# Logits read as pairs of neighbouring columns, six units with the one-table gate, and new instruction lists

## The chip, the core and the metric

The kernel runs on one NeuronCore of one Trainium2 chip. The metric is the device time of one execution in microseconds. Five engines work side by side, each through its own instruction list: PE multiplies matrices (its weight loads, PEld, overlap with it), DVE (VectorE), ACT (ScalarE) and POOL (GpSimd) work on rows, and SP issues the DMAs.

## The reference

A gated linear recurrence over 4 sequences of 5056 tokens with 256 channels, followed by a mixture of experts in which each of 32 slots (8 experts, 4 slots each) takes a weighted sum of all 20224 tokens:

```
a_t = exp(c * sigmoid(r_gate) * log(a_base))            # c = 8, a_base = sigmoid(a_param)
u   = sqrt(max(1 - a_t*a_t, 1e-6)) * sigmoid(i_gate) * x
y_t = a_t * y_(t-1) + u_t                               # over each sequence
logits = y @ phi                                        # 20224 x 32
d = softmax of logits over all tokens;  slot_input = d.T @ y
slot_out = relu(slot_input[e] @ w1[e]) @ w2[e]          # 8 experts, 256 -> 1024 -> 256
out = (softmax of logits over the 32 slots) @ slot_out  # 20224 x 256
```

All inputs and the output are fp32 in HBM: about 62 MB of x and gates, 17 MB of weights, 20.7 MB of output.

## The kernel before

The 20224 tokens are cut into 40 quads of 512 tokens (the last has 256), and the quads into 21 units: unit 0 is quad 0, units 1 to 19 hold two quads each (1024 tokens), unit 20 is quad 39. Units go by chunks of two, and units 0 to 17 pair up into groups of four (or three) quads for the softmax; units 18, 19 and 20 are groups of their own.

The loads put a quad into an `st` tile (gates) or half a `b` tile (x), a number of consecutive tokens in each partition. The recurrence needs channels in partitions, so everything is transposed on PE. For quad q, unit p, channel half h, group g the steps are, with the names of the instruction lists:

- SP: `Drq`, `Diq`, `Dxq` load the three inputs, `w1e` and `w2e` the weights, `ODg.j` writes output.
- `TRq` (PE, L742) transposes r_gate, `SRq` (ACT, L753) takes its tanh, `EXp.h` (ACT, L821) the exponential: a_t. `SQp.h` (POOL or DVE, L808) squares it, `RTp` (ACT, L844) takes the root.
- `SIq` (ACT, L766 or L768) is the input gate, `Uq` (POOL or DVE, L791) multiplies it with x, `TUp.h` (PE, L863) transposes the product into a PSUM pair, `STp.h` (DVE, L881) multiplies it with the root, `SCp.h` (DVE, L898) is the scan. y then stands in the unit's `b` tile, channels in partitions, token 8m+n of a two-quad unit in column 8m+n.
- `TYq` (PE, L921) transposes y back, eight 128x128 blocks for a quad, `YCq` (DVE L937 or ACT L935) copies it out of PSUM into a `yn` tile.
- `LGg.k` (PE, L980): the logits of a unit and channel half, four matmuls with 32 columns of phi as weights and y as the moving operand, into four strips of 32 partitions. `LEg` (DVE, L996) takes them out of PSUM with a running maximum, `LDg` (L1012, L1016) subtracts it, `TEg` (PE, L1027) transposes, `ESg` (ACT, L1036) is exp, `ACg.k` (PE, L1054) adds up the slot inputs over the tokens with y from `yn` as the moving operand, `AEg` (DVE, L1069) accumulates them.
- `CTg` (PE, L1428), `CMg`, `CSg`, `CEg`, `RRg`, `CNg`, `CHg`, `CLg` are the softmax over slots.
- When all tokens are scanned: `MX`, `MR`, `WJ`, `WE`, `W`, `SP`, `SL` merge the partial sums, `L1.e` and `L2.e` (PE, L1308 and L1356) are the experts, `SO` to `BD` (DVE, ACT) prepare slot_out, and then `HP`, `HE`, `OT` (PE, L1531), `OE` (DVE L1547 or ACT L1545) and `OD` make the output.

The input gate has kinds, one letter for each unit in `IV`. Kind S is a sigmoid, which needs a function table of its own on ACT; `U` multiplies it into the x tile and `TU` transposes that one tile. Kind E is tanh(i/2), which is in the table that the exponentials use; `U` multiplies it with x in the gate's own tile, and `TU` transposes both that tile and x and adds them up in PSUM (x + x tanh(i/2) is twice x sigmoid(i); the half goes into the root). So for E `TU` has 32 transposes of a unit for each two channel halves where S has 16, and the `st` tile of the gate is free after `TU`, where with S it is free after `U`. Kind P is tanh with a correction on POOL. There are 7 `st` tiles, which r_gate and i_gate share.

Nothing is ordered by chance: `ORDER` holds one list of step names for each engine, and each engine issues its steps in that order. A planner only assigns tiles and checks that the lists can run; the costs in `add(...)` calls don't reorder anything while `ORDER` is given. [...] `UD` and `SQD` say for which steps DVE may take over from POOL.

Of the kernel before, what the change touches and what calls it, by code (L numbers as in the profile page):

```python
# [17 lines left out]
P = 128  # L18
J = 4
# [10 lines left out]
IV = 'EEEESSSSPPESPSSSSSSSP'  # L30
# [43 lines left out]
SQD = 4  # L74
UD = 6
# [28 lines left out]
    ),  # L104
    "ACT": (
# [12 lines left out]
    ),  # L118
# [20 lines left out]
    ),  # L139
# [344 lines left out]
def kernel(  # L484
# [37 lines left out]
    def plen(p):  # L522
        return sum(qlen(q) for q in quads(p))
# [72 lines left out]
    def per_part(p):  # L596
        return plen(p) // P

    def token(v, p):
        return v.rearrange("c (p n) -> c p n", n=per_part(p))  # L600
# [1008 lines left out]
```

## Time and profile before

| | us |
|---|---|
| median of 3 runs (lowest, highest) | 310.09 (309.19, 310.15) |
| the profiled execution's own time | 310.56 |
| its span, first to last instruction | 308.8 |
| PE, DVE, ACT, POOL busy | 276.9, 252.1, 248.3, 201.8 |
| all inputs but weights loaded and scanned, merge done (SL) | about 232 |
| first output DMA issued | 255.2 |

The profile divides into three stages: up to 232 us the tokens are loaded, scanned and summed up; from 232 to 255 us the experts run, almost only on PE, and hardly any data is moved; from 255 us to the end the output is made and written. The busy time of an engine says little over the whole span, since each stage has its own limit; a row of a stage has to be read by itself. Quoted lines from the profile give times from the span's start; a group's row reads: line, engine, operation, output tile <- input tiles, shapes, count, then busy time and mean ns of one, then idle time before it and what ended it.

### The profile page before, as it was taken

How to read it: one execution, taken by the hardware profiler on the slowest of the kernel's cores; microseconds unless marked ns; L12 is line 12 of the kernel's file. 1: busy time of each engine (PE TensorE's matmuls, PEld its weight loads, DVE VectorE, ACT ScalarE, POOL GpSimd, SP SyncE). 2: the span in 40 equal slices, each digit the busy share in tenths (PEclk: the TensorE clock that was granted, in tenths of full speed). 3: DMA queues.
4: the chain of work that ended last, by engine and by line, in shares of the span. 5: the costliest groups of instructions: out<-in, count | busy, mean ns of one | idle time of the engine just before them, and what ended most of it. 6: DMA issues, size and time to landing. Idle time of an engine off the chain costs nothing.

```text
span 308.8 us, 6015 instructions
## 1 busy us (share of the span) xinstructions
PE 276.9 (90%) x2353; PEld 201.4 (65%) x2353; DVE 252.1 (82%) x295; ACT 248.3 (80%) x264; POOL 201.8 (65%) x149
## 2 busy tenths in 40 slices
PE   7989888978889999989889999999999989999960
PEld 6988676555556776766574567567654568788740
DVE  0275989899799899988999899999976988898620
ACT  5999999999999999899999999999460027755660
POOL 1542989888999996989597989793124656113200
PEclk9999999979999999999999999999997999999996
DMA  7999998999997677896988696799996008999996
GB/s 217 418 407 368 406 409 304 329 408 402 409 390 245 206 238 254 286 409 237 355 331 293 229 330 246 267 382 416 422 373 284 2 2 340 407 419 412 420 423 267
DMA packets 23776, 100.04 MB, mean 324 GB/s; under 512 B 2882, under 2 KB 2884, under 8 KB 19780
## 3 DMA queue, kind: packets, MB, share of 16 engines
q1 hardware_dynamic: 23744, 99.66, 84.2%
q8 instruction: 18, 0.29, 0.4%
q14 instruction: 10, 0.08, 0.1%
q10 hardware_dynamic: 4, 0.00, 0.0%
HBM read 78.94 MB, written 20.71 MB: 323 GB/s over the span
## 4 chain that ended last, share of the span: by engine, by line
PE 48%; DVE 22%; ACT 11%; POOL 7%; issue 5%; DMA 4%; ACTq 0%; DVEq 0%; POOLq 0%
PE one L980 9%; DVE b L898 8%; PE bank L1531 8%; PE pair L863 6%; PE pair L921 6%; DVE pair L881 5%; PE pair L742 5%; PE one L1531 4%; ACT b L753 3%; PE one L1054 3%; POOL b L791 3%; PE bank L1308 2%; ACT st L768 2%; POOL b L808 2%; DMA st<-in_r_gate_dram 2%
## 5 line engine op out<-in xcount | busy, mean ns | idle before, releaser
L808 POOL TENSOR_TENSOR b<-b 128x1024 f32<-128x1024 f32 (+2 forms) x38 | 68.8, 1833 | 20.5 <-ACT b L821 20.4
L791 POOL TENSOR_TENSOR b<-st,b 128x1024 f32<-128x1024 f32 (+1 forms) x29 | 67.7, 2347 | 12.3 <-DMA b<-in_x_dram 11.1
L881 DVE SCALAR_TENSOR_TENSOR pair<-b,pair 128x1024 f32<-128x1024 f32 (+2 forms) x42 | 48.3, 1156 | 7.5 <-PE pair L863 6.2
L742 PE MATMUL pair<-ident,st 128*128 128x128 f32 x316 | 44.0, 284 | 7.9 <-DMA st<-in_r_gate_dram 4.6
L742 PEld LDWEIGHTS pair<-ident,st 128*128 128x128 f32 x316 | 36.1, 145 | 18.9 <-issue 6.4
L863 PE MATMUL pair<-ident,b 128*128 128x128 f32 x316 | 44.3, 278 | 4.0 <-DVE b L898 1.8
L898 DVE TENSOR_TENSOR_SCAN b<-b,pair 128x1024 f32<-128x1024 f32 (+6 forms) x26 | 47.5, 1846 | 0.2
L921 PEld LDWEIGHTS pair<-ident,b 128*128 128x128 f32 x316 | 37.8, 193 | 12.4 <-issue 6.4
L898 DVE TENSOR_TENSOR_SCAN b<-b,b,pair 128x1024 f32<-128x1024 f32 (+2 forms) x22 | 45.5, 2074 | 0.2
L921 PE MATMUL pair<-ident,b 128*128 128x128 f32 x316 | 42.9, 281 | 2.0 <-DVE b L898 1.6
L863 PEld LDWEIGHTS pair<-ident,b 128*128 128x128 f32 x316 | 35.2, 141 | 14.1 <-issue 6.2
L753 ACT ACTIVATE b<-pair 128x1024 f32<-128x1024 f32 (+1 forms) x40 | 40.1, 1009 | 4.5 <-PE pair L742 4.1
L980 PE MATMUL one<-b,phi_sb 128*32 128x256 f32 (+1 forms) x328 | 41.7, 615 | 0.9 <-DVE b L898 0.8
L821 ACT ACTIVATE b<-b,ca 128x2048 f32<-128x2048 f32 (+3 forms) x24 | 42.0, 1791 | 0.0
L937 DVE COPY yn<-pair 128x1024 f32<-128x1024 f32 (+1 forms) x28 | 33.1, 1192 | 3.6 <-PE pair L921 3.4
L1531 PE MATMUL bank<-bd,hT 128*128 128x512 f32 x110 | 30.4, 400 | 0.7 <-ACT hT L1519 0.7
L1461 POOL TENSOR_TENSOR b<-b,rs_all 128x512 f32<-128x512 f32 (+3 forms) x12 | 10.8, 910 | 28.4 <-DVE rs_all L1453 19.4
L844 ACT ACTIVATE b<-b 128x2048 f32<-128x2048 f32 (+1 forms) x16 | 28.7, 1830 | 0.4 <-POOL b L808 0.3
L766 ACT ACTIVATE st<-st 128x1024 f32<-128x1024 f32 x24 | 24.1, 1051 | 0.1
L1054 PE MATMUL one<-yn,eS 128*32 128x257 f32 x312 | 23.3, 392 | 0.5 <-DVE b L996 0.3
L1531 PEld LDWEIGHTS bank<-bd,hT 128*128 128x128 f32 x110 | 19.8, 188 | 5.4 <-ACT hT L1519 1.4
L1545 ACT COPY b<-bank 128x512 f32<-128x512 f32 x27 | 15.6, 595 | 8.0 <-PE bank L1531 6.6
(137 smaller groups left out, 428.7 us busy)
## 6 DMA issues: line engine op xcount, KB each, us to landing
b<-in_x_dram SPq DMA_DIRECT2D x39, 512.0 KB, 6.9
st<-in_r_gate_dram SPq DMA_DIRECT2D x38, 512.0 KB, 6.4
st<-in_i_gate_dram SPq DMA_DIRECT2D x37, 512.0 KB, 5.7
out_dram<-b SPq DMA_DIRECT2D x17, 1024.0 KB, 6.8
b<-in_moe_w_dram SPq DMA_DIRECT2D x14, 1024.0 KB, 9.9
st<-in_moe_w_dram SPq DMA_DIRECT2D x4, 512.0 KB, 10.2
out_dram<-st SPq DMA_DIRECT2D x4, 512.0 KB, 2.9
b<-in_i_gate_dram SPq DMA_DIRECT2D x2, 512.0 KB, 8.3
```

Of the source, the lines that this page charges most:

```text
L742: nc.tensor.transpose(out=o[:, m, :], in_=raw("r", q)[:, m * D + h * P : m * D + (h + 1) * P], identity=ident,)
L753: nc.scalar.activation(dst, t(rp)[:, :, :c], AF.Tanh, scale=0.5)
L791: eng.tensor_tensor(out=o, in0=a, in1=b, op=ALU.mult)
L808: eng.tensor_tensor(out=t(Nb[p])[:, h, :c], in0=v, in1=v, op=ALU.mult)
L821: nc.scalar.activation(v, v, AF.Exp, scale=ca[:, h : h + 1], bias=ca[:, h : h + 1])
L863: nc.tensor.matmul(o[:, m, :], raw(nm, q)[:, m * D + h * P : m * D + (h + 1) * P], ident, is_transpose=True, start=(nm == nms[0] and m == ...
L881: nc.vector.scalar_tensor_tensor(v, w, 0.5e-3 if gate_of(quads(p)[0]) in "ED" else 1e-3, v, op0=ALU.max, op1=ALU.mult)
L898: nc.vector.tensor_tensor_scan(dst, dst, flat()[:, s0:s1], init, op0=ALU.mult, op1=ALU.add)
L921: nc.tensor.transpose(out=flat()[:, b * D + h * P : b * D + (h + 1) * P], in_=token(t(A[p])[:, h, : plen(p)], p)[:, :, i * J + b0 + b], id ...
L937: nc.vector.tensor_copy(out=dst, in_=v)
L980: nc.tensor.matmul(t(lp)[NS * j : NS * (j + 1), c0 : c0 + w].rearrange("s (i p) -> s i p", p=P), phi_sb[:, h, :], token(t(A[p])[:, h, : pl ...
L1531: nc.tensor.matmul(t(op), t(hT)[:, b * P // 2 : (b + 2) * P // 2], T["bd"][part].rearrange("p i d -> p (i d)"), start=(part == 0), stop=(p ...
```

## The change

1. The two quads of a unit share one token order. Before, quad i of a unit was the tokens 8m+4i to 8m+4i+3 of each partition m. Now, for units 3 and up, quad i is the tokens 8m+i, 8m+2+i, 8m+4+i, 8m+6+i, so the moving operand of a logits matmul is, for each m, two neighbouring columns of y instead of two columns that lie four apart, and the columns come out in the order (m, i) instead of (i, m). `TY`, `TE`, `CT` and `OE` pick their blocks accordingly (new function `cols`).
2. `IV`: units 4 and 5 (quads 7 to 10) go from kind S to kind E.
3. `SQD` from 4 to 6 and `UD` from 6 to 10: DVE may take SQ and U steps of more units. The planner's cost of a logits step is another number.
4. All five lists of `ORDER` are new.

```diff
-IV = 'EEEESSSSPPESPSSSSSSSP'
+IV = 'EEEEEESSPPESPSSSSSSSP'
...
-SQD = 4
-UD = 6
+SQD = 6
+UD = 10
...
-        "CA SQ0.1 SQ1.0 U0 SQ1.1 ST0.0 SC0.0 ST0.1 SC0.1 U2 ST1.0 SC1.0 SQ2.0 ST1.1 SC1.1 YC0.0 YC1.0 LE0 YC2.0 ST2.0 "
+        "CA SQ0.0 U0 SQ0.1 SQ1.0 SQ1.1 ST0.0 ST0.1 SC0.1 SC0.0 U1 U2 YC0.0 ST1.0 SC1.0 ST1.1 SC1.1 U3 U4 YC2.0 LE0 YC1.0 "
...
+    def cols(v, g, k):
+        p, i = unit[groups[g][k]]
+        c0 = (k - i) * P
+        if p < WIDE_FROM:
+            return v[:, k * P : (k + 1) * P]
+        return v[:, c0 : c0 + plen(p) // blocks(groups[g][k])].rearrange("q (p i) -> q i p", p=P)[:, i, :]
...
-                            in_=token(t(A[p])[:, h, : plen(p)], p)[:, :, i * J + b0 + b],
+                            in_=token(t(A[p])[:, h, : plen(p)], p)[:, :, (b0 + b) * len(quads(p)) + i if p >= WIDE_FROM else i * J + b0 + b],
...
+                        o = t(lp)[NS * j : NS * (j + 1), c0 : c0 + w]
+                        v = token(t(A[p])[:, h, : plen(p)], p)
+                        near = p >= WIDE_FROM
                         nc.tensor.matmul(
-                            t(lp)[NS * j : NS * (j + 1), c0 : c0 + w].rearrange("s (i p) -> s i p", p=P), phi_sb[:, h, :],
-                            token(t(A[p])[:, h, : plen(p)], p)[:, :, j::nb].rearrange("c p i -> c i p"),
+                            o.rearrange("s (p i) -> s p i", p=P) if near else o.rearrange("s (i p) -> s i p", p=P), phi_sb[:, h, :],
+                            v[:, :, j * w // P : (j + 1) * w // P] if near else v[:, :, j::nb].rearrange("c p i -> c i p"),
...
-                    out=t(ep)[:, k * rows : (k + 1) * rows], in_=t(lD)[:rows, k * P : (k + 1) * P], identity=ident[:rows, :rows]
+                    out=t(ep)[:, k * rows : (k + 1) * rows], in_=cols(t(lD)[:rows], g, k), identity=ident[:rows, :rows]
...
-                    out=t(cp)[:, k * rows : (k + 1) * rows], in_=lS(g)[:rows, k * P : (k + 1) * P], identity=ident[:rows, :rows]
+                    out=t(cp)[:, k * rows : (k + 1) * rows], in_=cols(lS(g)[:rows], g, k), identity=ident[:rows, :rows]
...
-                def e_oe(b0=at[j] + b0, op=op, og=ogs[j]):
-                    dst = t(og)[:, b0 * D : (b0 + 2) * D]
+                w = len(quads(unit[qs[j]][0])) if unit[qs[j]][0] >= WIDE_FROM else 1
+
+                def e_oe(b0=b0 * w + at[j], w=w, op=op, og=ogs[j]):
+                    dst = t(og).rearrange("p (n d) -> p n d", d=D)[:, b0 : b0 + w + 1 : w, :]
+                    src = t(op).rearrange("p (n d) -> p n d", d=D)
```

How the lists move instructions is shown at three places. In these rows the number behind a tile's name is its place in memory; line numbers are of the kernel before in the first fence and of the changed one in the second (L742 is there L749, L753 L760, L766 and L768 are L773 and L775, L844 L851, L863 L870, L935 L942, L980 L990, L1036 L1046).

The first place is the chunk of units 4 and 5. On ACT before, the gates SI7 to SI10 (L766, sigmoid) stand behind a table load, between the tanh steps of later r_gate quads, and the roots RT4 and RT5 (L844) behind another:

```order
L753 ACTIVATE b_75<-pair_91 128x2x512
L766 ACT_TABLE_LOAD
L766 ACTIVATE st_62<-st_62 128x1024
L753 ACTIVATE b_75<-pair_92 128x2x512
L766 ACTIVATE st_67<-st_67 128x1024
L766 ACTIVATE st_65<-st_65 128x1024
L753 ACTIVATE b_75<-pair_93 128x2x512
L766 ACTIVATE st_64<-st_64 128x1024
L844 ACT_TABLE_LOAD
L844 ACTIVATE b_74<-b_74 128x2048
L844 ACTIVATE b_76<-b_76 128x2048
```

ACT now at the same place:

```order
L760 ACTIVATE b_75<-pair_92 128x2x512
L775 ACTIVATE st_67<-st_67 128x1024
L775 ACTIVATE st_62<-st_62 128x1024
L775 ACTIVATE st_61<-st_61 128x1024
L760 ACTIVATE b_75<-pair_92 128x2x512
L851 ACT_TABLE_LOAD
L851 ACTIVATE b_72<-b_72,quarter 128x2048
L851 ACTIVATE b_70<-b_70,quarter 128x2048
```

The table load in front of the gates is gone, the gates are tanh, and the fourth of them (SI10) has moved behind the roots. On PE the transposes TU4.1 and TU4.0 with a logits step between them were, before:

```order
L863 MATMUL pair_92<-ident,b_69 128x128 x8
L980 MATMUL one_86<-b_71,phi_sb 32x256 x4
L863 MATMUL pair_91<-ident,b_69 128x128 x8
L1027 MATMUL one_86<-ident,lD_83 128x128 x4
L863 MATMUL pair_93<-ident,b_68 128x128 x8
```

And PE now, from TU4.1 (four rows) over the logits to TU4.0 (four rows):

```order
L870 MATMUL pair_91<-ident,st_62 128x128 x4
L870 MATMUL pair_91<-ident,b_72 128x128 x4
L870 MATMUL pair_91<-ident,st_67 128x128 x4
L870 MATMUL pair_91<-ident,b_72 128x128 x4
L1064 MATMUL one_87<-yn_79,eS_84 32x257 x4
L990 MATMUL one_86<-b_71,phi_sb 32x256 x4
L870 MATMUL pair_93<-ident,st_62 128x128 x4
L870 MATMUL pair_93<-ident,b_72 128x128 x4
L870 MATMUL pair_93<-ident,st_67 128x128 x4
L870 MATMUL pair_93<-ident,b_72 128x128 x4
```

Each TU step now reads the two gate tiles (`st`) as well as x (`b`), 16 transposes where there were 8.

The second place is the end of ACT's main work. Before, the roots of units 18 and 20 (b_70 and b_74) and then of 19 (b_72) stand behind one table load, with copies of y (L935) between them:

```order
L844 ACT_TABLE_LOAD
L844 ACTIVATE b_70<-b_70 128x2048
L844 ACTIVATE b_74<-b_74 128x2x256
L935 COPY yn_79<-pair_91 128x4x256
L935 COPY yn_81<-pair_92 128x4x256
L844 ACTIVATE b_72<-b_72 128x2048
L935 COPY yn_78<-pair_92 128x4x256
L1036 ACT_TABLE_LOAD
```

Now the roots of 18 and 19 come first:

```order
L851 ACT_TABLE_LOAD
L851 ACTIVATE b_75<-b_75 128x2048
L942 COPY yn_78<-pair_92 128x4x256
L851 ACTIVATE b_73<-b_73 128x2048
L942 COPY yn_79<-pair_92 128x4x256
L1046 ACT_TABLE_LOAD
```

And the exponentials and the root of unit 20 follow later, the root between two table loads of its own:

```order
L828 ACTIVATE b_72<-b_72,ca 128x256
L775 ACTIVATE st_64<-st_64 128x512
L942 COPY yn_79<-pair_91 128x4x256
L851 ACT_TABLE_LOAD
L851 ACTIVATE b_71<-b_71 128x2x256
L1457 ACT_TABLE_LOAD
```

Unit 20's exponentials and root have moved behind the roots of 18 and 19, and there is one more pair of table loads behind them.

The third place is the start of DVE's list (a scan is printed there as SCALAR_TENSOR_TENSOR at L898, now L905). Before, from the last scan of unit 0 on:

```order
L898 SCALAR_TENSOR_TENSOR b_68<-b_68,pair_93 128x512
L791 TENSOR_TENSOR st_66<-st_66,b_70 128x1024
L881 SCALAR_TENSOR_TENSOR pair_93<-b_70,pair_93 128x1024
L898 SCALAR_TENSOR_TENSOR b_69<-b_69,b_68,pair_93 128x1024
L808 TENSOR_TENSOR b_73<-b_71 128x1024
L881 SCALAR_TENSOR_TENSOR pair_92<-b_70,pair_92 128x1024
```

DVE now, from the last scan of unit 0 on:

```order
L905 SCALAR_TENSOR_TENSOR b_68<-b_68,pair_92 128x512
L798 TENSOR_TENSOR st_65<-st_65,b_70 128x1024
L798 TENSOR_TENSOR st_63<-st_63,b_70 128x1024
L944 COPY yn_78<-pair_91 128x4x256
L888 SCALAR_TENSOR_TENSOR pair_92<-b_70,pair_92 128x1024
L905 SCALAR_TENSOR_TENSOR b_68<-b_68,pair_92 128x1024
L888 SCALAR_TENSOR_TENSOR pair_91<-b_70,pair_91 128x1024
L905 SCALAR_TENSOR_TENSOR b_68<-b_68,pair_91 128x1024
L798 TENSOR_TENSOR st_62<-st_62,b_70 128x1024
L798 TENSOR_TENSOR st_67<-st_67,b_70 128x1024
```

The products U1, U3 and U4 stand here beside U2 (L798), and further on U7 and U8; POOL had all but U2 before. The square SQ2.0 (L808) has gone to POOL, and SQ0.0, ahead of these rows, has come from POOL.

More of the change, by code (lines that the diff above doesn't have):

```diff
@@ L986, in mk_group @@
                 own = lg is None
-                lg = add("PE", f"LG{g}.{2 * gunits[g].index(p) + h}", w * 0.00195 * (0.6 if nb == 2 else 1.0),
+                lg = add("PE", f"LG{g}.{2 * gunits[g].index(p) + h}", w * (0.00205 if p >= WIDE_FROM and w > P else 0.0039),
                          deps=[SC[(p, h2)] for h2 in range(h + 1)] + [ld[("x", PHI)]], gate=begun(lg),
@@ L1497 @@
                 og_of[p] = ogs[-1]
-            at.append(jj * J if two else 0)
+            at.append(jj if two else 0)
         done = {j: [] for j in range(n)}
@@ L1540 @@
                 own = at[j] + b0 == 0
-                def e_oe(b0=at[j] + b0, op=op, og=ogs[j]):
-                    dst = t(og)[:, b0 * D : (b0 + 2) * D]
+                w = len(quads(unit[qs[j]][0])) if unit[qs[j]][0] >= WIDE_FROM else 1
+                def e_oe(b0=b0 * w + at[j], w=w, op=op, og=ogs[j]):
+                    dst = t(og).rearrange("p (n d) -> p n d", d=D)[:, b0 : b0 + w + 1 : w, :]
+                    src = t(op).rearrange("p (n d) -> p n d", d=D)
                     if planner.cur.eng_used == "ACT":
-                        nc.scalar.copy(out=dst, in_=t(op))
+                        nc.scalar.copy(out=dst, in_=src)
                     else:
-                        nc.vector.tensor_copy(out=dst, in_=t(op))
+                        nc.vector.tensor_copy(out=dst, in_=src)
                 x_ = add(("DVE", "ACT"), f"OE{g}.{a0 + b}", 0.60, deps=[k], prio=pr + b * 0.1,
```

114 rows, old and new, of the table ORDER are left out of this document.

## The prediction

> **What bounds the kernel now.** I read the stages first (busy time of each engine, in brackets its instructions), cut where ACT ends its main work and where the merge and the first output begin.
>
> ```profile
> core 0: us, PE busy (x) PEld busy (x) DVE busy (x) ACT busy (x) POOL busy (x), PEclk, DMA share, GB/s
> 0.00:20.00 20.00, 17.89 (x139) 17.19 (x139) 5.96 (x8) 16.17 (x17) 8.29 (x31) 1.00 0.90 338
> 20.00:206.00 186.00, 168.51 (x1467) 119.21 (x1467) 170.85 (x145) 180.98 (x155) 160.28 (x87) 0.99 0.87 323
> 206.00:232.00 26.00, 25.25 (x247) 17.18 (x245) 23.81 (x38) 18.01 (x29) 8.60 (x7) 1.00 1.00 403
> 232.00:254.00 22.00, 20.87 (x283) 12.33 (x284) 17.32 (x39) 1.76 (x4) 13.02 (x13) 0.92 0.23 93
> 254.00:309.00 55.00, 44.39 (x223) 35.50 (x221) 34.15 (x69) 31.37 (x61) 11.62 (x13) 0.95 0.92 377
> ```
>
> From 20 to 206 us ACT is busy for 180.98 of 186 us. PE, with 90% of the whole span the busiest on the page, has 17.5 us free there, DVE 15.2. So ACT sets the pace and PE mostly follows. From 206 to 232 it is PE (25.25 of 26) with DVE close behind; the experts up to 254 are PE's alone; the last stage moves data at 92% of the DMA engines. The timeline shows the hand-over at 206:
>
> ```profile
> 203.69 2.43 ACT L844 ACTIVATE b<-b 128x2048 f32<-128x2048 f32 x2
> 206.15 1.23 DVE L881 SCALAR_TENSOR_TENSOR pair<-b,pair 128x1024 f32<-128x1024 f32 x1
> 224.47 0.74 DVE L898 TENSOR_TENSOR_SCAN b<-b,b,pair 128x256 f32<-128x256 f32 x1
> 225.13 1.20 DVE L937 COPY yn<-pair 128x1024 f32<-128x1024 f32 x1
> 231.73 0.23 DVE L1271 COPY yn<-bank 128x64 f32<-128x64 f32 x1 [1.01 <-PE bank L1274]
> ```
>
> ACT's roots of units 18 and 20 end at 206.12, ST18.0 starts on DVE at once, the last scan ends at 225.2, and SL lets the experts start at 231.96. So the time is: ACT's work up to RT18, plus some 26 us of DVE and PE, plus two stages that the change hardly touches. What stands in ACT's way up to 206, and in DVE's up to 232, the lists of waits tell (total, times, longest; first three rows ACT):
>
> ```profile
> ACT b L753 <- PE pair L742: 4.1, 6, 1.9
> ACT st L768 <- DMA st<-in_i_gate_dram: 0.9, 1, 0.9
> ACT eS L1036 <- PE one L1027: 0.6, 1, 0.6
> DVE pair L881 <- PE pair L863: 6.2, 9, 1.8
> DVE yn L937 <- PE pair L921: 3.4, 4, 2.1
> DVE b L996 <- PE one L980: 2.1, 3, 1.1
> ```
>
> PE costs ACT 4.7 us, of which 1.9 is the first load at the start, which stays; so 2.8 are in reach.
>
> **Logits on PE.** Rows of groups, shapes kept apart (the x16 row is unit 0, from a window around 34 us; the x8 row is unit 20, around 226 us):
>
> ```profile
> L980 PE MATMUL one<-b,phi_sb 128*32 128x256 f32 x304 | 40.2, 635 | 0.9 <-DVE b L898 0.8
> L1054 PE MATMUL one<-yn,eS 128*32 128x257 f32 x312 | 23.3, 392 | 0.5 <-DVE b L996 0.3
> L980 PE MATMUL one<-b,phi_sb 128*32 128x128 f32 x16 | 1.1, 404 | 0.0
> L980 PE MATMUL one<-b,phi_sb 128*32 128x128 f32 x8 | 0.7, 283 | 0.0
> L863 PE MATMUL pair<-ident,b 128*128 128x128 f32 x316 | 44.3, 278 | 4.0 <-DVE b L898 1.8 <-POOL b L791 1.8 <-ACT b L753 0.2
> ```
>
> A logits step is 8 records, so 304 are 38 steps of 1.06 us. An AC step has the same form, but its moving operand is contiguous: 312 records are 39 steps of 0.60 us. What differs is the step between the columns. Unit 0 reads y at 16 bytes, unit 20 at 8 bytes, both 128 columns: 404 against 283 ns, and a transpose with 128 contiguous columns of the identity takes 278. So 8 bytes run like contiguous ones and 16 don't. The change gives pairs at 4 bytes with 28 bytes to the next pair, which no row shows. Bounds: nothing (the mean step is 16 bytes), or the whole 0.46 us. I take the whole, since the row it is nearest to is unit 20's, where two of the columns also share 16 bytes. [...] Units 3 to 19 have 34 steps: 34 x 0.46 = 15.6 us less PE.
>
> **Units 4 and 5 as kind E.** 32 more transposes at 44.3/316 = 0.14 us are 4.5 us more PE, around 45 to 75 us, where PE has a tenth of its time free. PE saves 11 us in all. What ACT gains is in these rows:
>
> ```profile
> L844 ACT ACT_TABLE_LOAD x10 | 12.8, 1283 | 0.2
> L935 ACT COPY yn<-pair 128x1024 f32<-128x1024 f32 x12 | 12.0, 1010 | 1.5 <-PE pair L921 0.8 <-ACT b L844 0.4 <-ACT b L1447 0.3
> L821 ACT ACTIVATE b<-b,ca 128x256 f32<-128x256 f32 x2 | 1.1, 610 | 0.0
> L1043 ACT ACTIVATE dm<-M 128x1 f32<-128x1 f32 x10 | 2.9, 286 | 0.0
> L844 ACT ACTIVATE b<-b 128x2048 f32<-128x2048 f32 x15 | 28.2, 1911 | 0.4 <-POOL b L808 0.3
> L844 ACT ACTIVATE b<-b,quarter 128x2048 f32<-128x2048 f32 x4 | 7.9, 1994 | 0.0
> ```
>
> Up to the end of RT18 ACT's list has one table load less (-1.28), one copy of y more (five instead of four, +1.01), not yet the two exponentials of unit 20 (-1.22) and one dm (-0.29), and two roots of the slower form (2 x 0.083, +0.17): **-1.6 us** of work on the engine that sets the pace. Further on, one pair of table loads comes for unit 20's root; from 206 to 232 ACT has 8 us free, so I cost it at nothing. If that cover is gone, ST20 starts late by up to 2.6 us.
>
> Of the 2.8 us that ACT waits for PE, I count half, **-1.4**: from 20 to 206 us PE has 28 logits steps to shorten (-12.9) and 4.5 more to do, but a transposition waits as much for its tile or its r_gate load as for PE's turn. Bounds are 0 and -2.8.
>
> **From RT18 to the merge.** Before, the copy at 225.13 (YC37) stands between the last scan and LE11; it goes to ACT, 1.20 off DVE. PE has four wide logits steps less to wait for, 1.8 us. But DVE gets a three-instruction RR0 between WJ and W, and PE two CT steps ahead of the merge product, where both wait for WE or AE11. I take **-1.1**, with bounds 0 and -3.0.
>
> **Moved at nothing.** TE and CT read their weights at 8 bytes: a load at 32 bytes (TY) takes 193 ns, a contiguous one 145, so 68 of them cost 0 to 3.3 us of PEld, which is busy 65% and lies beside PE. OE writes runs of 256 floats as before. SP's order is new, the bytes are the same.
>
> ```profile
> L921 PEld LDWEIGHTS pair<-ident,b 128*128 128x128 f32 x316 | 37.8, 193 | 12.4 <-issue 6.4 <-DVE b L898 3.4 <-ACT b L753 1.5
> L742 PEld LDWEIGHTS pair<-ident,st 128*128 128x128 f32 x316 | 36.1, 145 | 18.9 <-issue 6.4 <-DVE b L898 5.9 <-ACT st L768 1.9
> 210.91 17.72 SPq L1213 DMA_DIRECT2D b<-in_moe_w_dram  x8
> b<-in_moe_w_dram SPq DMA_DIRECT2D x14, 1024.0 KB, 9.9
> ```
>
> What is late next is the weights: the last is issued at 228.6 and by the median lands 9.9 us later, at 238.5, an estimate; L2.0, which needs it, starts at 240.6. If the tiles for them don't come free earlier, a gain beyond 2 us stops there. But they come free by the same steps that end sooner, and the last weight is now for L2.4, four steps on.
>
> DVE gets U1, U3, U4, U7, U8 and SQ0.0 and gives up SQ2.0 and one copy before RT18:
>
> ```profile
> 15.41 1.22 DVE L791 TENSOR_TENSOR st<-st,b 128x1024 f32<-128x1024 f32 x1
> 31.46 2.21 DVE L808 TENSOR_TENSOR b<-b 128x1024 f32<-128x1024 f32 x1
> ```
>
> Five at 1.22 less a square and a copy are about +4 us, if a product meets no POOL step; the same kind of instruction, SQ2.0, took 2.21 where POOL was working. Five at 2.21 make it +9. DVE has 15.2 us free up to 206, so this is covered either way, though the second leaves little. POOL has 25.7 us free there and gains nothing by giving the products away.
>
> The sum against the profiled execution (310.56, its span 308.8 and 1.8 around it): 310.56 - 1.6 - 1.4 - 1.1 = 306.5. That execution lies 0.47 above the median of 310.09, so against the median it is **306.0**. Its own range, from the bounds of the terms: 302.7 to 308.5.
>
> **Rivals.**
> - The gain is larger. The chain of waits puts the logits steps on the path:
>
> ```profile
> by line: PE one L980 9.1%; DVE b L898 8.2%; PE bank L1531 8.0%; PE pair L863 6.3%; PE pair L921 6.1%; DVE pair L881 5.2%; PE pair L742 4.8%; issue 4.6%; PE one L1531 3.7%; ACT b L753 3.2%; PE one L1054 3.0%; POOL b L791 3.0%; PE bank L1308
> ```
>
>   9.1% of 308.8 is 28 us, of which 0.46/1.06 would go, 12 us, less 4.5 for TU: 302, or somewhat less with the table load. Against it: while the chain runs through PE, ACT is at 97%, and ACT's work alone can't end more than 1.6 + 5 us earlier. It gives about 301.5. Chance 0.14.
> - DVE takes over as the bound. The products moved there meet POOL's reads. [...] The mechanism here: with five times 1 us on both engines, and DVE's own waits for PE (11.7 us) not shortened, DVE needs up to 9 of its 15 free us and reaches ST18 no earlier than now. Then only part of the end remains: about 309.3. Decides from some 6 us of lost DVE time. Chance 0.14.
> - Slower: the gates of quads 7 to 10 hold their `st` tiles until TU instead of U, and the r_gate loads of the next chunk wait for them. The chain has such a wait, and the transposes of r_gate wait for those loads now and then:
>
> ```profile
> 67.97 5.99 DMA st<-in_r_gate_dram
> L742 PE MATMUL pair<-ident,st 128*128 128x128 f32 x316 | 44.0, 284 | 7.9 <-DMA st<-in_r_gate_dram 4.6
> ```
>
>   ACT had other work then. One more of 5.99 us that ACT can't fill costs 6.0 - 4.1: 312. It decides from 4.1 us of new idle time on ACT. Chance 0.11.
> - The pairs are read no faster. Then PE has 4.5 us more to do and saves nothing; if all of that reaches the path, 310.1 + 4.5 - 1.6 is 313. Chance 0.05.
>
> **How the numbers follow.** My forecast has 0.56. A change within 0.3% (309.2 to 311.0) can't be told from none. Faster: 0.54 of the first, 0.14, and a third of DVE's case: 0.73. Same: most of DVE's case and a little of the others, 0.12. Slower: 0.15. The range 301.5 to 311.0 leaves out the slower cases (0.15) and a little below.
>
> **What would show it.** In the new profile: logits groups with 256 columns at about 0.6 us a step and 392 ns a record (unchanged 635 would end this argument); no table load ahead of the gates of units 4 and 5; ACT's RT18 ends near 203; SL near 227.6; the waits of ACT for L749 under 3 us; the output stage still 54 us long. Wrong would make it: ACT below 95% from 20 us to RT18, a DVE without gaps from 25 us on, or experts that wait for a weight.

## The result and the profile after

The changed kernel takes 307.85 us (median of 20 runs, 306.19 to 311.16) against 310.12 (20 runs, 308.91 to 312.03): a ratio of 0.992, with a 95% interval of 0.9896 to 0.9943. It is faster by 2.3 us where 4.1 were forecast. The ratio and its interval leave out runs over 1.5% above the fastest of their kernel, such as the one of 311.16 us. The profiled execution shown here took 308.2 us, its span is 305.5. The stages, cut at the same times as before, with the same columns:

```profile
0.00:20.00 20.00, 17.12 (x129) 16.14 (x129) 7.07 (x10) 16.12 (x17) 3.52 (x29) 1.00 0.91 338
20.00:206.00 186.00, 163.80 (x1558) 126.89 (x1559) 179.00 (x152) 184.81 (x159) 154.76 (x83) 1.00 0.90 335
206.00:232.00 26.00, 23.19 (x242) 14.96 (x245) 22.30 (x44) 16.14 (x28) 7.52 (x9) 0.93 0.93 378
232.00:254.00 22.00, 20.29 (x256) 13.21 (x249) 18.29 (x42) 4.89 (x11) 13.73 (x14) 1.00 0.12 46
254.00:306.00 52.00, 40.24 (x198) 31.30 (x196) 28.07 (x54) 27.59 (x54) 8.64 (x11) 0.94 0.94 386
```

From 20 to 206 us ACT (fourth bracket) now works 184.81 of 186 us, where it worked 180.98: it bounds this stage almost without a gap. The groups that the change is about, from the list by shape:

```profile
L990 PE MATMUL one<-b,phi_sb 128*32 128x256 f32 x304 | 24.7, 423 | 0.0
L990 PE MATMUL one<-b,phi_sb 128*32 128x128 f32 x24 | 1.9, 366 | 0.0
L870 PE MATMUL pair<-ident,st 128*128 128x128 f32 x104 | 16.0, 276 | 1.4 <-ACT b L760 0.7 <-DVE st L798 0.4 <-ACT yn L942 0.3
L798 DVE TENSOR_TENSOR st<-st,b 128x1024 f32<-128x1024 f32 x7 | 8.5, 1221 | 6.5 <-DMA b<-in_x_dram 3.7 <-ACT st L775 2.7
L851 ACT ACT_TABLE_LOAD x11 | 14.1, 1283 | 0.2
```

A logits record with 256 columns takes 423 ns on the mean instead of 635 (398 from 100 to 200 us, where all are read as pairs), all 304 of them together 24.7 us instead of 40.2. The third row holds the transposes of gate tiles, 104 with those of units 4 and 5. Seven products are on DVE now, at 1.22 us each: POOL's timeline has it idle or just at the end of a step at each of them, and none took longer than 1.23 us.

What ACT and DVE wait for (total, times, longest; ACT up to its last root of the main stage, DVE from 20 to 206 us):

```profile
ACT b L760 <- PE pair L749: 2.7, 3, 1.9
ACT ca L1096 <- PE one L1091: 0.4, 1, 0.4
ACT st L775 <- DMA st<-in_i_gate_dram: 0.4, 1, 0.4
DVE st L798 <- ACT st L775: 2.7, 2, 1.4
DVE rm L1451 <- PE one L1438: 1.2, 1, 1.2
DVE pair L888 <- PE pair L870: 1.2, 2, 0.7
DVE yn L944 <- PE pair L928: 0.2, 1, 0.2
```

DVE waited 11.7 us for PE before (6.2, 3.4 and 2.1), and waits 2.6 now: 1.2 for a step CT (L1438), 1.2 for the transposes TU and 0.2 for TY. The hand-over from the main stage to the experts, from the timelines of ACT, DVE, PE and POOL:

```profile
197.39 1.92 ACT L851 ACTIVATE b<-b 128x2048 f32<-128x2048 f32 x1
199.34 2.36 DVE L888 SCALAR_TENSOR_TENSOR pair<-b,pair 128x1024 f32<-128x1024 f32 x2 [0.22 <-ACT b L851]
216.63 0.75 DVE L905 TENSOR_TENSOR_SCAN b<-b,b,pair 128x256 f32<-128x256 f32 x1
222.36 0.83 POOL L1471 TENSOR_TENSOR b<-b,rs_all 128x384 f32<-128x384 f32 x1 [9.00 <-DVE rs_all L1463]
222.57 2.91 DVE L1265 TENSOR_SCALAR W<-R,wj 128x128 f32<-128x128 f32 x1 [0.29 <-ACT wj L1264]
223.13 0.53 POOL L1240 MEMSET yn<- 128x512 f32 x1
223.60 1.80 POOL L1298 MEMSET b<- 128x2048 f32 x1
226.14 0.66 PE L1271 MATMUL bank<-W,accS 128*128 128x32 f32 x4 [2.10 <-DVE accS L1079]
227.10 0.23 DVE L1281 COPY yn<-bank 128x64 f32<-128x64 f32 x1 [0.42 <-PE bank L1284]
```

RT18 ends at 199.31, where the roots of units 18 and 20 ended at 206.12, and ST18.0 starts 6.8 us earlier. The last scan ends at 217.4, 7.8 us earlier. But SL, which lets the experts start, ends at 227.33 against 231.96: 3.2 us of the gain are gone in between. The place is W (L1265), a small step that takes 2.91 us here, while POOL runs CN0 and then the two fills SZ and HZ. Before, it took 0.28:

```profile
230.05 0.28 DVE L1255 TENSOR_SCALAR W<-R,wj 128x128 f32<-128x128 f32 x1
```

In POOL's new list CN0 stands ahead of the fills, and it waits 9.00 us for RR0, so the fills come just when DVE does W. After the experts, something is lost again:

```profile
243.74 1.05 PE L1366 MATMUL one<-st,b 128*32 128x256 f32 x16
244.33 2.26 DVE L1475 TENSOR_SCALAR st<-b 128x512 int32<-128x512 int32 x2
246.51 0.41 DVE L1475 TENSOR_SCALAR yn<-b 128x512 int32<-128x512 int32 x1
246.84 0.47 DVE L1385 TENSOR_SCALAR hs<-one,rd 128x256 f32<-128x256 f32 x1
247.37 0.70 PE L1388 MATMUL bank<-hs,R 128*128 128x256 f32 x2 [1.39 <-DVE hs L1385]
249.57 1.62 PE L1541 MATMUL bank<-bd,hT 128*128 128x512 f32 x6
```

The last L2 product ends at 244.8, but SO (L1385) starts only at 246.84, since DVE takes its list in order and CH6, CH2 and CH5 (L1475) stand ahead of it. In sum, with the earlier trace's times from its own timeline: the main stage gains 6.8 us; from there to SL 2.2 are given back (25.84 us before, 28.02 after), from SL to the first output product 0.8 (21.4 and 22.2), and in the output stage 0.5 (55.4 and 55.9). What is left of the 6.8 is the 3.3 us that the span is shorter.

### The profile page after: what moved, and what is told of

It reads as the page before. It is cut to its first block, busy times and chain, and to the rows that moved or that the text cites. A ratio compares the mean times of both kernels' runs of the same rounds, so it can differ in the third digit from the quotient of the medians.

```text
span 305.5 us, 6049 instructions
## 1 busy us (share of the span) xinstructions
PE 264.6 (87%) x2371; PEld 202.5 (66%) x2371; DVE 254.7 (83%) x299; ACT 249.6 (82%) x266; POOL 188.2 (62%) x144
## 4 chain that ended last, share of the span: by engine, by line
POOL 23%; ACT 22%; PE 17%; DMA 14%; DVE 11%; issue 9%; SPq 1%; POOLq 0%; DVEq 0%
POOL b L798 10%; POOL b L815 9%; PE bank L1541 8%; DMA b<-in_x_dram 6%; DMA st<-in_i_gate_dram 5%; ACT b L828 4%; ACT b L760 4%; ACT b L851 4%; DVE b L905 3%; DMA out_dram<-b 2%; ACT st L773 2%; DVE pair L888 2%; ACT st L775 2%; POOL st L798 2%; PE one L1318 2%
## 5 line engine op out<-in xcount | busy, mean ns | idle before, releaser
L815 POOL TENSOR_TENSOR b<-b 128x1024 f32<-128x1024 f32 (+1 forms) x38 | 68.5, 1826 | 38.5 <-ACT b L828 33.2
L798 POOL TENSOR_TENSOR b<-st,b 128x1024 f32<-128x1024 f32 (+1 forms) x25 | 58.0, 2335 | 1.4 <-ACT st L773 1.1
L749 PE MATMUL pair<-ident,st 128*128 128x128 f32 x316 | 42.8, 281 | 11.6 <-DMA st<-in_r_gate_dram 5.7
L905 DVE TENSOR_TENSOR_SCAN b<-b,pair 128x1024 f32<-128x1024 f32 (+6 forms) x28 | 52.2, 1883 | 0.5
L749 PEld LDWEIGHTS pair<-ident,st 128*128 128x128 f32 x316 | 35.1, 143 | 18.9 <-DVE b L905 4.7
L870 PE MATMUL pair<-ident,b 128*128 128x128 f32 x316 | 43.9, 275 | 2.4 <-DVE b L905 1.2
L760 ACT ACTIVATE b<-pair 128x1024 f32<-128x1024 f32 (+1 forms) x40 | 39.5, 1008 | 2.8 <-PE pair L749 2.7
L905 DVE TENSOR_TENSOR_SCAN b<-b,b,pair 128x1024 f32<-128x1024 f32 (+2 forms) x20 | 40.8, 2048 | 0.3
L870 PEld LDWEIGHTS pair<-ident,b 128*128 128x128 f32 x316 | 35.3, 141 | 7.7 <-issue 2.2
L1541 PE MATMUL bank<-bd,hT 128*128 128x512 f32 x122 | 32.9, 403 | 1.9 <-DVE hT L1531 1.8
L944 DVE COPY yn<-pair 128x1024 f32<-128x1024 f32 (+1 forms) x26 | 30.5, 1193 | 0.8 <-PE pair L928 0.8
L1529 ACT CAST hT<-bank 128x512 fp32r<-128x512 f32 (+1 forms) x11 | 6.2, 570 | 28.0 <-PE bank L1518 23.4
L990 PE MATMUL one<-b,phi_sb 128*32 128x256 f32 (+1 forms) x328 | 26.5, 418 | 0.1
L1478 POOL TENSOR_TENSOR st<-b,st 128x512 f32<-128x512 f32 (+3 forms) x11 | 11.8, 1083 | 22.8 <-DVE st L1475 19.9
L851 ACT ACTIVATE b<-b 128x2048 f32<-128x2048 f32 (+1 forms) x14 | 25.0, 1816 | 0.1
```

The costliest lines, as they stand in the source:

```text
L749: nc.tensor.transpose(out=o[:, m, :], in_=raw("r", q)[:, m * D + h * P : m * D + (h + 1) * P], identity=ident,)
L760: nc.scalar.activation(dst, t(rp)[:, :, :c], AF.Tanh, scale=0.5)
L798: eng.tensor_tensor(out=o, in0=a, in1=b, op=ALU.mult)
L815: eng.tensor_tensor(out=t(Nb[p])[:, h, :c], in0=v, in1=v, op=ALU.mult)
L851: nc.scalar.activation(v, v, AF.Sqrt, bias=quarter if f != 1.0 else f, scale=-f)
L870: nc.tensor.matmul(o[:, m, :], raw(nm, q)[:, m * D + h * P : m * D + (h + 1) * P], ident, is_transpose=True, start=(nm == nms[0] and m == ...
```

## The experiments

Each kernel ran in turn with the kernel before; ratios are to it, with their 95% interval.

**The parts of the change by themselves.** The first kernel has the shared token order alone, with the lists and the planner's numbers of before. Against the changed kernel that is, beside the lists:

```diff
-IV = 'EEEEEESSPPESPSSSSSSSP'
+IV = 'EEEESSSSPPESPSSSSSSSP'
-SQD = 6
-UD = 10
+SQD = 4
+UD = 6
```

> The kernel before with the shared token order alone: logits read as pairs, old lists, old gate kinds. Theory 1 (the shorter logits steps take away waits of ACT and DVE for PE): ACT's last main root (RT18) ends 1.5 to 3 us earlier than 206.1, the last scan 2 to 4 us earlier, total about 307 (306 to 308.5). Rival (the lists make the gain; PE was off the path while ACT is at 97%): logits records go from 635 to about 423 ns all the same, PE gets idle, but the total stays at 309.5 to 310.5.

The second is the kernel before with one line changed, the six one-table units:

```diff
-IV = 'EEEESSSSPPESPSSSSSSSP'
+IV = 'EEEEEESSPPESPSSSSSSSP'
```

> The kernel before with units 4 and 5 as kind E alone: old lists, old token order. Theory 1: one table load less on ACT (-1.3) against 32 more transposes on a PE that still has the long logits steps (+4.5 of its time, part of it on the path): 309 to 311. Rival (the gates hold their st tiles longer, r_gate loads come late): 312 or more, with a longer wait of the r_gate transposes for their loads than 4.6 us.

The third has both, the first kernel's pairs and this line, with all old lists:

> Pairs and kind E for units 4 and 5, with all old lists. Theory 1: about the sum of the two single changes, 305.5 to 308, so the lists add little. Rival (the lists make the gain): 309 to 311, and RT18 ends no earlier than 204.

The fourth is the changed kernel with the token order of before in TY, LG, TE, CT and OE (and the old planner cost of LG, which reorders nothing); so it has the new lists and gates and no pairs. Its logits product:

```diff
-                            o.rearrange("s (p i) -> s p i", p=P) if near else o.rearrange("s (i p) -> s i p", p=P), phi_sb[:, h, :],
-                            v[:, :, j * w // P : (j + 1) * w // P] if near else v[:, :, j::nb].rearrange("c p i -> c i p"),
+                            t(lp)[NS * j : NS * (j + 1), c0 : c0 + w].rearrange("s (i p) -> s i p", p=P), phi_sb[:, h, :],
+                            token(t(A[p])[:, h, : plen(p)], p)[:, :, j::nb].rearrange("c p i -> c i p"),
```

> The changed kernel with the old token order: new lists and kind E, but logits read columns four apart again (1.06 us a step). Theory 1: 34 steps of 0.4 us more on PE, of which lists made for short steps can hide little: 311 to 316, with ACT again waiting for PE by some us before RT18. Rival (the lists make the gain): 307.5 to 309.

| kernel | time | ratio | RT18 starts | span |
|---|---|---|---|---|
| before | | 1 | 203.7 | 308.8 |
| pairs alone | 307.02 | 0.9883 (0.9834 to 0.9933) | 200.4 | 304.4 |
| gates alone | 314.49 | 1.0128 (1.0079 to 1.0178) | 205.7 | 310.3 |
| both, old lists | 309.37 | 0.9963 (0.9931 to 0.9994) | 204.0 | 308.7 |
| changed, without pairs | 312.85 | 1.0088 (1.0051 to 1.0125) | 200.8 | 309.8 |
| changed (all) | 307.85 | 0.992 (0.9896 to 0.9943) | 197.4 | 305.5 |

(The first four were timed beside a median of 310.34 for the kernel before.) The pairs alone bring 1.2%; that is more than the whole change by the ratios, but the two intervals overlap. Taking them out of the changed kernel costs 1.7%. In the kernel with pairs alone the trace lists no wait of ACT for PE from 20 to 206 us, where it waited 2.8 us before (2.2 for the transposes of r_gate and 0.6 for an exponent tile), and RT18 starts 3.3 us earlier. The logits row is the same as in the changed kernel:

```profile
L990 PE MATMUL one<-b,phi_sb 128*32 128x256 f32 x304 | 25.4, 424 | 0.9 <-DVE b L905 0.5 <-DVE b L1454 0.3
```

The one-table gates, which I had costed at a small gain for ACT, slow the kernel by 1.3% alone and by 0.8% beside the pairs. The new lists (with the new `SQD` and `UD`) take about half of the latter back; the intervals with the old lists and with the new ones overlap at their ends. The next step was to find why the gates cost, and what the new lists give away at the end.

**Why the gates cost.** In the kernel with gates alone ACT works less in the window from 20 to 110 us, although it has a table load less to do there. First the row of before, then of the kernel with gates alone (ACT's busy time, PEclk, DMA share, GB/s):

```profile
20.00:110.00 90.00, 88.50 (x73) 0.98 0.93 354
```

```profile
20.00:110.00 90.00, 84.31 (x70) 1.00 0.91 345
```

It stands idle 5.7 us instead of 1.5, 4.2 of them behind the transposes of r_gate (0.9 before). Those wait for their loads (6.5 us instead of 3.1 in this window), and the loads wait in SP's queue. In the next three fences the rows are the loads of r_gate of quad 16, i_gate of quad 13, x of quad 19 and r_gate of quad 15. SP's issues before:

```profile
54.58 0.38 SPq L669 DMA_DIRECT2D st<-in_r_gate_dram  x1
55.05 0.38 SPq L669 DMA_DIRECT2D st<-in_i_gate_dram  x1
55.48 0.42 SPq L669 DMA_DIRECT2D b<-in_x_dram  x1
56.50 0.33 SPq L669 DMA_DIRECT2D st<-in_r_gate_dram  x1
```

and with gates alone:

```profile
53.71 0.33 SPq L669 DMA_DIRECT2D st<-in_r_gate_dram  x1
58.63 0.33 SPq L669 DMA_DIRECT2D st<-in_i_gate_dram  x1
59.00 0.66 SPq L669 DMA_DIRECT2D b<-in_x_dram  x1
62.03 0.33 SPq L669 DMA_DIRECT2D st<-in_r_gate_dram  x1
```

The i_gate load of quad 13 has no tile until 58.63, and the r_gate load of quad 15 behind it goes out 5.5 us later than before. The waits of SP for TU (L863) rise from 4.8 to 9.7 us in this window: the tiles that a TU step must read are freed by it, and no longer by the products U. Three kernels put this to the test. One reorders two loads in the kernel with both and the old lists:

```diff
-... Dr14 Di11 Dr16 Di13 Dx19 Dr15 Di12 ...
+... Dr14 Dr16 Dr15 Di11 Di13 Dx19 Di12 ...
```

> The kernel with pairs, the six one-table units and the old lists (309.37), with one edit in SP's list: the r_gate loads of quads 16 and 15 stand directly behind that of quad 14, ahead of the i_gate loads of quads 11 and 13 (before: Dr14 Di11 Dr16 Di13 Dx19 Dr15; now: Dr14 Dr16 Dr15 Di11 Di13 Dx19). Theory 3 (the one-table gates cost because their tiles are held until TU: SP, which takes its list in order, stands before the i_gate load of quad 13 until a TU of units 4 or 5 has read a gate tile, 4 to 5 us, and the r_gate loads behind it come late): the load of quad 15 is issued near 55 us instead of 61.9, ACT's waits for PE between 70 and 110 us fall from 2.7 to under 1.5 us, and the time falls by 1 to 2.5 us, to about 307.5. Rival: what costs is that seven gate tiles are too few whatever the order; then the wait only moves from the r_gate loads to the i_gate loads (ACT waits for these 3.4 us now), and the time stays at 309.4 within 0.5 or rises. Second rival: the gates' cost is not in these loads but in PE's eight more transposes a TU step; then nothing changes.

It measured 310.84 us, a ratio of 1.0007 (0.9968 to 1.0047), no better than 0.9963. Quad 15's load did go out near 55 us, but the two i_gate loads behind it now started at 59.43, and ACT's waits from 20 to 110 us were 5.3 us where they were 6.1. My expectation missed, and the rival "seven tiles are too few whatever the order" fits. So the next kernel has eight:

```diff
-N_ST = 7
+N_ST = 8
-        T["hs"] = [sb.tile([P, FJ], F32, name=f"hs{i}") for i in range(4)]
+        T["hs"] = [x[:, :FJ] for x in [*T["eS"], *T["lD"]]]
```

> Pairs, six one-table units and the old lists again (ratio 0.9963 to the kernel before; with pairs alone it was 0.9883), now with eight gate tiles (N_ST 8) instead of seven; the four hs tiles of the merge lie in the tiles eS and lD, which are done with by then, to make room. Theory 3 (the one-table gates cost since they hold gate tiles until TU): with the eighth tile SP no longer stands 4 to 5 us before the i_gate load of quad 13; ACT's waits between 20 and 206 us fall from 6.3 us to 3.5 or less, RT18 starts at 202 or earlier instead of 204.0, and the ratio comes to 0.988 to 0.992. Rival (seven tiles are not the limit; PE's longer TU steps or the order of ACT's list are): RT18 stays at 204 and the ratio at 0.995 to 0.998.

It took 306.63 us, a ratio of 0.9895 (0.9859 to 0.9932): 0.7% below the one with seven tiles, whose interval (0.9931 to 0.9994) it overlaps only at the end. RT18 starts at 201.0 instead of 204.0. SP's issues at the same place:

```profile
53.30 0.34 SPq L676 DMA_DIRECT2D st<-in_r_gate_dram  x1
54.17 0.33 SPq L676 DMA_DIRECT2D st<-in_i_gate_dram  x1
54.55 0.42 SPq L676 DMA_DIRECT2D b<-in_x_dram  x1
58.65 0.33 SPq L676 DMA_DIRECT2D st<-in_r_gate_dram  x1
```

Quad 13's i_gate load goes out at 54.17 instead of 58.50, and quad 15's r_gate load behind it at 58.65 instead of 61.92. ACT's waits fell less than expected, from 6.3 to 4.0 us between 20 and 203 us (3.5 was my bound). An eighth tile may help a kernel without the new gates as well; that control was not run. The other half of the cost, PE's longer TU steps, was tried without the tiles: in the kernel with pairs alone, the TU steps of units 4 and 5 are made twice.

```diff
-                    for nm in nms:
+                    for nm in (("x", "x") if p in (4, 5) else nms):
```

> The kernel with pairs alone (old lists, four one-table units, ratio 0.9883) with the transposes of the four TU steps of units 4 and 5 made twice, 16 a step instead of 8, into the same place (the second pass overwrites the first with the same values): PE's added work of the one-table gates without their tiles, some 4.5 us of PE at 45 to 75 us. Theory 3: these transposes are covered: the ratio stays at 0.988, within 0.3%, and RT18 near 200.4. Rival (they are what the one-table gates cost under the old lists, because the transposes of the r_gate steps queue behind them on PE): ACT waits 2 us or more longer for PE before 110 us, RT18 starts at 203 to 204, and the ratio is 0.994 to 0.998.

It took 305.82 us (the kernel before 309.86 beside these two), a ratio of 0.9862 (0.9823 to 0.9902), not slower than without them (0.9883). ACT is busy 89.32 us in the window where the kernel with gates alone had 84.31:

```profile
20.00:110.00 90.00, 89.32 (x75) 1.00 0.93 358
```

So beside the pairs the added transposes are covered, and what the gates cost there fits the tiles that they hold, as the eighth tile gives back 0.7 of the 0.8%. Why they cost more without the pairs (1.3%) was not tested. In the changed kernel itself ACT has 89.25 of 90 us there and waits 0.4 for the transposes. Its lists as a whole hide the cost; which of their edits does it was not isolated, and the one small edit of SP's list that I tried does not.

**What the new lists give away at the end.** Two edits of the changed kernel, one in POOL's list and one in DVE's, and both together:

```diff
-U39 CN0 SZ HZ CN5 ...
+U39 SZ HZ CN0 CN5 ...
```

> The changed kernel with one edit in POOL's list: the two fills SZ and HZ stand ahead of CN0. Theory 2 (the hand-over gives back what the main stage gained): in the changed kernel W on DVE took 2.91 us (0.28 before) while POOL's fill HZ (1.80 us, from 223.60) ran beside it, because POOL waited 9 us for RR0 in front of CN0. With the fills ahead, W is back at about 0.3 us, SL comes near 225.0 instead of 227.1, and the time falls by 1.5 to 2.1 us, to about 306. Rival: the experts' products or DVE's later list (CH6, CH2, CH5 ahead of SO) decide when the output starts; then SL is earlier all the same, the first output step stays at 249.6, and the time stays at 307.9 within 0.5. Second rival: W took long for another reason than the fill, and is still 2.9 us.

```diff
-CH6 CH2 CH5 SO CS11 SH ...
+CH6 SO CH2 CH5 CS11 SH ...
```

> The changed kernel with one edit in DVE's list: SO stands behind CH6 instead of behind CH6, CH2 and CH5. Theory 2: L2 ended at 244.8, but SO started only at 246.84, since DVE takes its list in order and the two steps CH6 and CH2 took 2.26 us; SO now starts near 245.5, PE's wait for it (1.4 us) goes, and the first output step comes 1.0 to 1.4 us earlier (near 248.4): a time of 306.5 to 306.9. Rival: the first output step waits for the transposes HP, and through them for CH2 and CH5 (which now come later): no gain, 307.6 to 308.2.

> Both edits of the two kernels before it in this call. Theory 2: the two add up, since they lie one behind the other on the path: the output starts 3 to 3.5 us earlier than in the changed kernel, near 246.3, and the time is 304.4 to 305.2. Rival: the output stage (55.9 us from its first product to the end in the changed kernel) is bound by something else than its start, and grows by what the start gains: 306.5 or more.

| kernel | time | ratio | SL ends | SO starts | first output product |
|---|---|---|---|---|---|
| changed | 307.85 | 0.992 (0.9896 to 0.9943) | 227.33 | 246.84 | 249.6 |
| fills first | 306.02 | 0.9846 (0.9793 to 0.9899) | 225.62 | 243.54 | 246.3 |
| SO first | 306.78 | 0.9891 (0.9843 to 0.9939) | 228.67 | 248.19 | 250.9 |
| both | 304.94 | 0.9812 (0.9763 to 0.986) | 227.10 | 244.35 | 247.1 |

(The three were timed beside a median of 309.64 for the kernel before. The profiled executions of the three were 0.3, 0.8 and 1.7 us later at RT18 than that of the changed kernel, so columns are to be compared from RT18 on.) With the fills ahead of CN0, W takes 0.22 us again, and HZ lies ahead of it:

```profile
219.72 1.81 POOL L1298 MEMSET b<- 128x2048 f32 x1
223.08 0.22 DVE L1265 TENSOR_SCALAR W<-R,wj 128x128 f32<-128x128 f32 x1
225.39 0.23 DVE L1281 COPY yn<-bank 128x64 f32<-128x64 f32 x1 [0.32 <-PE bank L1284]
```

The time falls as expected, by the ratios 0.7% or 2.3 us, though the two intervals still touch. Both rivals, that the output start would not move and that W took long for another reason, are out. With SO behind CH6, PE's wait for it is halved (1.39 to 0.72 us). In the profile of that kernel alone the output starts no earlier, at 250.9 where 248.4 was expected; TensorE's granted clock was 0.50 to 0.59 there from 228 to 234 us, so that profile can't show what the edit is worth. With both edits the time falls by 1.1% or 3.3 us, to 304.94 where 304.4 to 305.2 was expected:

```profile
242.50 1.93 DVE L1475 TENSOR_SCALAR st<-b 128x512 int32<-128x512 int32 x1
244.35 0.46 DVE L1385 TENSOR_SCALAR hs<-one,rd 128x256 f32<-128x256 f32 x1
244.87 0.70 PE L1388 MATMUL bank<-hs,R 128*128 128x256 f32 x2 [0.72 <-DVE hs L1385]
```

SO's edit alone is 0.3% by the ratios, within what the intervals leave open; with both, the gain over the changed kernel is outside of them. From W to the first output product it takes 27.0 us in the changed kernel, 23.3 before, and 22.5 with both edits; the first two hold a fall of the granted clock worth about 1.6 us each (last section), the third does not. The kernel with both edits, at 304.94 us, beats both the kernel before and the changed one.

## Why the prediction was right, and where it was not

The forecast was 306.0 us and faster; it is 307.85, faster, and within the wide range of 301.5 to 311.0. The mechanism, shorter logits steps and less waiting of ACT for PE, is borne out by the kernels with and without the pairs. That the sum came near is in part luck: terms that were too small and terms that were missing cancelled. SL came at 227.33 where I had 227.6, but only because ACT ended its main work 3.7 us earlier than forecast (199.3 for 203) and the stretch from there to SL was 3.3 us longer.

- **Logits at the full 0.46 us a step: right.** The 304 records take 24.7 us instead of 40.2, 15.5 less where I had 15.6. Four of the 38 steps, those of units 1 and 2, are read as before at 1.06 us; the other 34 come to 0.60 each. The row it was nearest to, unit 20's at 8 bytes, was the right one to choose: the trace has 423 ns against 635. That two columns share 16 bytes was my reason to choose it; no run shows why pairs are read faster. The rival that pairs are no faster is out.
- **ACT's work and waits up to RT18, -1.6 and -1.4: too small.** ACT's busy time up to the last root ahead of the hand-over, before and then after:

```profile
0.00:206.12 206.12, 197.28 (x171) 0.99 0.87 324
```

```profile
0.00:199.32 199.32, 194.28 (x168) 1.00 0.90 336
```

  ACT does 3.0 us less and stands idle 3.8 us less. Of the work, I had left out the root of unit 20 (0.61), which stood ahead of that time before; some 0.8 us I can't place, as records overlap in part. Of the 2.8 us of waits for PE that I had in reach, 2.0 went where I counted half: those for the r_gate transposes fell from 4.1 to 2.7, the one for an exponent tile (0.6) went. Waits that I had counted as staying shrank too: for the first ca, a wait for PE that my 4.7 us had left out (1.1 to 0.4), for an i_gate load (0.9 to 0.4) and for POOL's square (0.3). The pairs alone moved RT18 by 3.3 us, more than my bound of 2.8. One reading was wrong besides: ST18.0 did not start "at once" behind ACT's roots. RT18 itself had ended at 205.61, and DVE ran a step LE, for whose logits it had waited, until ST18.0:

```profile
205.47 0.75 DVE L996 TENSOR_SCALAR_CACHE_REDUCE b<-one,M 128x512 f32<-128x512 f32 x1 [0.44 <-PE one L980]
```

  Now ST18.0 waits 0.22 us for RT18.
- **Units 4 and 5 as kind E at no cost: right for the changed kernel as a whole, wrong as a step.** The transposes are covered, as I said. The tiles are not: my slower rival named that mechanism, and under the old lists the gates cost 0.8% beside the pairs, of which an eighth tile gives back 0.7, and 1.3% without them. I gave it 0.11 and missed that the lists decide it. With the new ones ACT waits 0.4 us for these transposes between 20 and 110 us.
- **From RT18 to the merge, -1.1: wrong.** It came out +2.2. DVE's path to the last scan is 1.0 us shorter (19.1 to 18.1), but I did not look at what POOL does at that time. I had costed POOL's list at nothing, and it held W for 2.6 us. Nor was the gain there without that: with the fills first the same stretch takes 26.1 us, since RR0, which I had named, stands ahead of W, and the fill now lies over the step MR (1.58 us instead of 0.22 in the changed kernel).
- **Experts and output at nothing: nearly right.** 0.8 and 0.5 us were lost. The weights, which I named as late next, stop nothing: the edit of POOL's list moved the experts 1.7 us forward, and the first output product followed by 3.3 (1.6 of them by the clock, below).
- **DVE does not take over.** Its waits for PE fell from 11.7 to 2.6 us, which my rival took as not shortened, and the seven products ran at 1.22 us each. The 1 us on both engines that this rival counted is in the trace of before, at one place: DVE's square of 31.46 us took 2.21 instead of 1.22, and of POOL's three squares from 28.72 us on, which lie over it, the last took 2.88 where the other two took 1.89. DVE is near its limit all the same, busy 179.0 of 186 us.
- **The larger gain, 301.5: not reached.** The part of the chain through the logits was not worth its share: the pairs alone moved RT18 by 3.3 us where this rival took 12, and in the changed kernel ACT's work fills 99% of the stage.

## What to carry to other kernels

When one engine sets the pace, look at the small steps of the hand-over to the next stage before costing a new order at nothing: write down for each of them what the other engines run at that moment. A tile that is read one step later on is a change to the load queue too; count the tiles of that kind, and ask which load stands behind the one that finds none. And split a change that has several parts: here one part alone gave about as much as the whole.

## What was not expected of the hardware

- A short step of DVE lasted through several steps of POOL on end, fills among them: in the changed kernel W started at 222.57 us, while CN0 ran (222.36 to 223.19), and ended at 225.48, when CN0, SZ and HZ (to 225.40) had. W took 2.90 to 2.91 us in the three kernels in which POOL's list has CN0 right ahead of the fills SZ and HZ (the changed one, the one without pairs, the one with SO first), and 0.22 to 0.28 in the three others looked at (before, fills first, both edits). A step CH (L1475, 128x512) took 0.41 us at 250.41 in the changed kernel, where POOL was idle, and 2.10 at 247.33 in the kernel before (L1465 there), where POOL was at work; that link was seen in the timelines only. What holds W is not shown beyond that. I had weighed such an overlap for the products U alone.
- The granted clock of TensorE fell to about a half for some 4 us or more at the start of the experts in four of the twelve profiled executions. First the changed kernel from 228 to 232 us, then the one with the fills first (PE's busy time, PEclk, DMA share, GB/s):

```profile
228.00:232.00 4.00, 4.00 (x52) 0.57 0.58 197
```

```profile
228.00:232.00 4.00, 4.00 (x66) 1.00 0.86 291
```

  The first 64 products of L1 took 5.46 us there instead of 3.89. The kernel before shows the same fall (0.57 from 232 to 236 us), and so do those with both parts and the old lists (0.50 from 232 to 234) and with SO first (0.50 from 228 to 232); the one with pairs alone and the one with both edits of the lists don't. So 1.6 of the 3.3 us between these two profiled spans are the clock and not the edit, and the timed 2.3 us are the better measure. PE had idled 2.1 us just ahead of it in the changed kernel, but 2.2 in the one without pairs, which kept its full clock (1.00), and only 0.4 in the kernel before, which did not; what sets it off stays open.
